# Scales of a weight matrix from sums of absolute values on ScalarE, where maxima on VectorE gave them

## The chip, the cores and the metric

The kernel runs on one core of a Trainium2 chip. The core has five engines, which run side by side and wait for each other through semaphores: TensorE (PE, matrix products; its weight loads are listed apart as PEld), VectorE (DVE), ScalarE (ACT), GpSimd (POOL) and SyncE (SP, which here issues nearly all DMAs). Each engine takes its instructions from a queue, in order. The metric is the time of one execution on the device in microseconds, lower being better, as a median over runs.

## The reference

Local and global attention for 8 sequences with 8 heads, followed by a feed-forward network:

```
k_all, v_all = concat(k_g, k_l), concat(v_g, v_l)        # 32 global + 512 local keys, head size 64
out_g = softmax(q_g @ k_all.T / 8) @ v_all               # 32 global queries see all
s     = concat(q_l @ k_g.T / 8, where(|i - j| <= 32, q_l @ k_l.T / 8, -1e9))
out_l = softmax(s) @ v_all                               # 512 local queries
x = concat(out_g, out_l) as [4608, 512]
h = x @ w_in                                             # w_in [512, 2048]
g = where(h > 0, h, exp(min(h, 0)) - 1)
return g @ w_out                                         # w_out [2048, 512]
```

The activations are float32; the two weight matrices come as float64.

## The kernel before

**Precision.** The two products of the network are done in f16, with each float32 operand split into a high and a low f16 part, and three products (high x high, high x low, low x high). For the split an operand is first divided by a power of two, so that it fits the range of f16. `unit` does it for one slice of weights: `power` keeps the exponent bits of a measure of the slice's size, `inverse` makes the reciprocal of it times a constant, ACT writes the high part (L216) and DVE the low part (L219). The powers stand in `pww` (for w_in) and `pwo` (for w_out), and every later scale is computed from them: `tables` multiplies the two and takes the largest product of a group of slices, `scales` makes from it the factors that are applied to the network's values. So any power of two that is large enough gives a correct split, as long as these tables use the same one.

**The weights.** Both matrices are read as pairs of 32-bit words (they come as float64), 1 MB at a time: eight slices of w_in and eight of w_out, in turn, w_in first. Each such slice is one `unit`. `fetch` loads it into the tile `raw`, of which there are two buffers, so the fetch of one unit waits until all instructions on the raw tile of the unit two before are done. A unit's steps are:

- s0: ACT takes absolute values of the high words (L188), POOL clamps them (L189);
- s1a, s1b, s1c: DVE builds the float32 number from high and low words (L193, L196, L200); the last reads the raw low words;
- s1d: the size of the slice. For w_in (m == 0) DVE takes the maximum of the absolute values in each partition (L205). For w_out ACT takes absolute values, writes them over the raw low words, and sums them in each partition on the way (L207); the sum is at least the maximum, and it serves as the measure;
- s2: for w_in alone, PE transposes the column of measures and DVE takes its maximum over the partitions (`all_max`, L141 and L142), as one power is used for all rows of a slice of w_in;
- s3 and s4: the power, the high part (L216) and the low part (L219).

**Order.** The program is written as one long stream of steps. `attention` yields after each small piece of attention work, `ffn_stream` after each small piece of the network, and the loop at the end mixes the two by a table, `PACE`. Each piece advances a clock by one tick; `defer(n, fn)` puts a step n ticks later. A unit's steps are put 1 to 5 ticks apart in the lead (the first 66 pieces of attention, with no network work yet) and up to 9 ticks later, the size at 5 or 9; s2 follows 8 ticks (w_out) or 17 ticks (w_in) after the unit's start. Units start at fixed pieces in the lead (`UNITS`) and then after every 14 pieces (`CONV`). The fetch of a unit is written one unit ahead. From this stream a planner makes the queue of each engine: it goes by the order of the program, but lets a later instruction pass an earlier one that would not be ready by its model of costs. DMA issues of SyncE stand in one queue: k, q and v of the attention, the raw weights (L174), and partial outputs of the network (`od`, L443 and L462), as blocks of rows are begun before all weights are converted.

**Around the change.** While weights are converted, DVE also does the scores' mask and minimum (L783), the sums for softmax (L793, L794, L798), the transposed probabilities (L814 or ACT), the low part of x (L574), the ELU (L345) and the low part of g (L348), and adds partial outputs (L458). ACT does the exponentials of the scores (L789), three passes over h for the ELU (L336 to L338), the high part of g (L352) and of x (L571), and copies out of PSUM (L749 to L753, L862). PE does scores (L772, L706), transposes by an identity matrix (L812, L745 to L748, L141), the products with v (L856, L825, L892), and the network (L327, L450; from the moment that all weights are there, L485, with seven products in place of eight).

Of the kernel before, what the change touches and what calls it, by code (L numbers as in the profile page):

```python
# [10 lines left out]
F32 = mybir.dt.float32  # L11
F32R = mybir.dt.float32r
I32 = mybir.dt.int32
AF = mybir.ActivationFunctionType
ALU = mybir.AluOpType
AX = mybir.AxisListType
# [44 lines left out]
def attn_ffn(ctx: ExitStack, tc: tile.TileContext, qT, qgT, kT, vT, vgT, vpT, w_in, w_out, mask, out):  # L61
    nc = tc.nc
# [22 lines left out]
    def defer(n, fn):  # L85
        if n == 0:
            return fn()
        later.setdefault(now[0] + n, []).append(fn)
# [39 lines left out]
    def power(dst, src):  # L128

        dst = dst.bitcast(I32)  # L130
        nc.vector.tensor_scalar(dst, src.bitcast(I32), 0x7f800000, None, ALU.bitwise_and)
        nc.vector.tensor_scalar_max(dst, dst, LOW)

    def inverse(dst, src):

        nc.vector.tensor_scalar(dst.bitcast(I32), src.bitcast(I32), TOP, -1.0, ALU.subtract, ALU.mult)

    def all_max(dst, src):

        tp = ps_a.tile([P, 512], F32, name="pa")  # L140
        tc.keep_in_program_order(nc.tensor.transpose(tp[:, 0:P], src.to_broadcast([P, P]), ident))  # L141
        nc.vector.tensor_reduce(out=dst, in_=tp[:, 0:P], op=ALU.max, axis=AX.X)  # L142
# [34 lines left out]
    def unit(m, p, raw):  # L177
        f = slice(2 * p * P, 2 * (p + 1) * P)
        shape = [P, NC, 2 * P] if m == 0 else [P, 2, DM]
        parts = [w[:, :, f] for w in win] if m == 0 else [w[:, 2 * p:2 * p + 2, :] for w in wout]  # L180
        pw = (pww if m == 0 else pwo)[:, p:p + 1]
        u = ffn.tile(shape, F32, name="cu", bufs=3)
        mx = ffn.tile([P, 4], F32, name="cm", bufs=4)
        high, low = raw[..., 1], raw[..., 0]
        ui = u.bitcast(I32)

        def s0():
            nc.scalar.activation(u, high.bitcast(F32), AF.Abs)  # L188
            nc.gpsimd.tensor_scalar(u, u, FMAX, FMIN, ALU.min, ALU.max)  # L189

        def s1a():
            tc.keep_in_program_order(
                nc.vector.tensor_scalar(ui, ui, 3, 0x3ffffff8, ALU.logical_shift_left, ALU.bitwise_and))  # L193

        def s1b():
            nc.vector.scalar_tensor_tensor(out=ui, in0=high, scalar=-0x40000000, in1=ui,  # L196
                                           op0=ALU.bitwise_and, op1=ALU.bitwise_or)

        def s1c():
            nc.vector.scalar_tensor_tensor(out=ui, in0=low, scalar=29, in1=ui,  # L200
                                           op0=ALU.logical_shift_right, op1=ALU.bitwise_or)

        def s1d():
            if m == 0:
                nc.vector.tensor_reduce(out=mx[:, 0:1], in_=u, op=ALU.max, axis=AX.XY, apply_absolute_value=True)  # L205
            else:
                nc.scalar.activation(low.bitcast(F32), u, AF.Abs, accum_out=mx[:, 1:2])  # L207

        def s2():
            if m == 0:  # L210
                all_max(mx[:, 1:2], mx[:, 0:1])

        def s3():
            power(pw, mx[:, 1:2])
            inverse(mx[:, 3:4], pw)
            nc.scalar.activation(parts[0], u, AF.Copy, scale=mx[:, 3:4])  # L216

        def s4():
            nc.vector.scalar_tensor_tensor(out=parts[1].rearrange("p a b -> p (a b)") if m else parts[1],  # L219
                                           in0=u.rearrange("p a b -> p (a b)") if m else u, scalar=mx[:, 3:4],  # L220
                                           in1=parts[0].rearrange("p a b -> p (a b)") if m else parts[0],
                                           op0=ALU.mult, op1=ALU.subtract)

        d = 1 if lead[0] else 2
        lag = 7 if m else 16
        for i, fn in ((1, s0), (1 + d, s1a), (1 + 2 * d, s1b), (1 + 3 * d, s1c), (1 + 4 * d, s1d),
                      (1 + lag, s2), (2 + lag, s3), (3 + lag, s4)):
            defer(i, fn)
# [848 lines left out]
```

## Time and profile before

| | |
|---|---|
| median of 3 runs | 960.44 us (958.44 to 963.3) |
| the profiled execution | 964.03 us |
| its span, first to last instruction | 962.2 us |
| PE, DVE, ACT, POOL busy | 914.8, 738.6, 661.9, 273.1 us |
| mean granted clock of TensorE | 0.97 |
| read from and written to HBM | 70.89 and 15.20 MB |

Times in the profile count from the start of the span. An engine is busy while it executes; waiting and issuing of DMAs are not counted. The granted clock is the share of TensorE's full clock that it was allowed in a stretch. In a timeline a row is start, length, engine, line, operation, what is written and read, shapes, and in brackets the idle time of the engine before it and the instruction that ended it. The chain of waits is followed back from the last instruction, at each step to what released it. Lines such as L205 are those of the kernel before.

### The profile page before, as it was taken

Reading aid. Unit: us, or ns where it says so; the run is one execution under the profiler, and the core shown is the slowest. Engines: PE = TensorE matmul, PEld = TensorE weight load, DVE = VectorE, ACT = ScalarE, POOL = GpSimd, SP = SyncE. Lnnn points to the kernel's source line nnn. Section 1 sums busy time; section 2 is a strip of 40 time slices with the busy share of each in tenths; the row PEclk is TensorE's granted clock in tenths of the full one; section 3 lists DMA queues with packets and bytes.
Section 4 is the critical chain, followed back from the end, with each engine's and each line's share of the span. In section 5 each row is a group of like instructions: output and inputs, shape, how many; then the busy total and the mean of one; then the engine's idle time right before and its main releaser. Section 6 shows DMA issues by size and latency. Waiting matters only on the chain.

```text
span 962.2 us, 23824 instructions
## 1 busy us (share of the span) xinstructions
PE 914.8 (95%) x9216; PEld 730.1 (76%) x9216; DVE 738.6 (77%) x2033; ACT 661.9 (69%) x1568; POOL 273.1 (28%) x483
## 2 busy tenths in 40 slices
PE   5887889899999999999999999999999999999997
PEld 2655566566666788788888888888888888888886
DVE  4877889989977876778776868687777877676566
ACT  4666788775676767757776866776776767666564
POOL 3636275372632212221221212222242222110000
PEclk7779899989999999999999999999999999999999
DMA  7852676622343114101230023001410101000000
GB/s 266 276 178 91 228 256 219 209 78 67 121 145 109 41 59 141 48 26 45 90 134 25 25 99 121 27 27 52 148 68 25 46 24 34 1 23 23 1 23 22
DMA packets 41769, 87.64 MB, mean 91 GB/s; under 512 B 7736, under 2 KB 8888, under 8 KB 41656
## 3 DMA queue, kind: packets, MB, share of 16 engines
q1 hardware_dynamic: 41368, 85.85, 26.4%
q8 instruction: 73, 1.20, 0.5%
q14 instruction: 40, 0.33, 0.1%
q10 hardware_dynamic: 288, 0.26, 0.1%
HBM read 70.89 MB, written 15.20 MB: 89 GB/s over the span
## 4 chain that ended last, share of the span: by engine, by line
PE 67%; DVE 17%; ACT 8%; issue 3%; POOL 3%; DMA 1%; DVEq 0%; SPq 0%; ACTq 0%; POOLq 0%
PE pa L327 25%; PE acc L485 12%; PE h L485 9%; PE pa L825 4%; PE acc L450 3%; PE pa L772 3%; PE h L327 3%; PE pa L812 2%; ACT p L789 2%; DVE gl L348 2%; PE pa L892 2%; DVE cu L278 1%; POOL p L796 1%; PE pa L706 1%; DVE cu L196 1%
## 5 line engine op out<-in xcount | busy, mean ns | idle before, releaser
L327 PEld LDWEIGHTS <-winh 128*128 128x128 f16 x2160 | 210.0, 99 | 42.0 <-issue 10.8
L796 POOL TENSOR_SCALAR p<-p,sm 128x128 f32<-128x128 f32 x256 | 144.1, 580 | 317.8 <-DVE sm L794 167.2
L327 PE MATMUL pa<-xh,winh 128*128 128x256 f16 x824 | 224.9, 273 | 0.1
L327 PE MATMUL pa<-xh,winl 128*128 128x256 f16 x824 | 224.6, 273 | 0.0
L327 PE MATMUL pa<-xl,winh 128*128 128x256 f16 x824 | 224.6, 273 | 0.0
L364 ACT ACTIVATE gh<-gx,xs 128x896 f16<-128x896 f32 x103 | 107.3, 1042 | 123.2 <-DVE gx L361 123.1
L348 DVE SCALAR_TENSOR_TENSOR gl<-gx,xs,gh 128x896 f16<-128x896 f32 x103 | 119.5, 1160 | 60.0 <-ACT gh L364 59.1
L485 PEld LDWEIGHTS <-gh 128*128 128x128 f16 x1456 | 139.6, 98 | 24.0 <-issue 7.4
L789 ACT ACTIVATE p<-p,m 128x160 f32<-128x160 f32 x256 | 106.6, 420 | 42.9 <-DVE m L783 41.3
L327 PEld LDWEIGHTS <-winl 128*128 128x128 f16 x1080 | 106.4, 99 | 14.5 <-issue 1.2
L336 ACT ACTIVATE g<-pa,xs 128x512 f32<-128x512 f32 x103 | 70.4, 683 | 24.1 <-PE pa L327 23.4
L485 PE MATMUL acc<-wouth,gh 128*128 128x256 f16 x312 | 85.2, 273 | 0.0
L485 PE MATMUL acc<-woutl,gh 128*128 128x256 f16 x312 | 85.0, 273 | 0.0
L485 PE MATMUL acc<-wouth,gl 128*128 128x256 f16 x312 | 85.0, 273 | 0.0
L338 ACT ACTIVATE g<-g 128x512 f32<-128x512 f32 x135 | 85.0, 630 | 0.0
L485 PEld LDWEIGHTS <-gl 128*128 128x128 f16 x728 | 71.2, 98 | 9.2 <-DVE gl L348 1.0
L327 PE MATMUL h<-xh,winh 128*128 128x256 f16 x256 | 71.9, 282 | 4.1 <-ACT hs L337 3.1
L485 PE MATMUL h<-raw,gh 128*128 128x256 f16 x416 | 75.0, 273 | 0.0
L327 PE MATMUL h<-xl,winh 128*128 128x256 f16 x256 | 71.8, 281 | 0.7 <-DVE xl L574 0.7
L327 PE MATMUL h<-xh,winl 128*128 128x256 f16 x256 | 71.8, 281 | 0.0
L783 DVE CUSTOM_DVE_ANT_0 p<-pa,msk 128x160 f32<-128x160 f32 x228 | 61.0, 317 | 7.1 <-PE pa L772 5.3
L345 DVE SCALAR_TENSOR_TENSOR gx<-g,hs 128x512 f32<-128x512 f32 x51 | 35.9, 705 | 36.0 <-ACT g L338 35.7
(237 smaller groups left out, 2028.8 us busy)
## 6 DMA issues: line engine op xcount, KB each, us to landing
k<-kT SPq DMA_DIRECT2D x32, 640.0 KB, 5.1
v<-vT SPq DMA_DIRECT2D x64, 256.0 KB, 2.7
q<-qT SPq DMA_DIRECT2D x32, 256.0 KB, 5.6
raw<-w_in SPq DMA_DIRECT2D x8, 1024.0 KB, 6.4
raw<-w_out SPq DMA_DIRECT2D x8, 1024.0 KB, 5.5
out<-o SPq DMA_DIRECT2D x32, 256.0 KB, 2.3
od<-o SPq DMA_DIRECT2D x24, 256.0 KB, 3.3
o<-od SPq DMA_DIRECT2D x24, 256.0 KB, 2.8
```

The source lines that it names most:

```text
L327: nc.tensor.matmul(h[:, j, :], wt[:, c, f], xt[:, c, :], start=k == 0, stop=k == 11)
L336: nc.scalar.activation(g, hf, AF.Relu, scale=sc[:, p:p + 1])
L338: nc.scalar.activation(g, g, AF.Exp, scale=-1.0)
L345: nc.vector.scalar_tensor_tensor(out=out, in0=ins[0], scalar=-1.0, in1=ins[1], op0=ALU.add, op1=ALU.max)
L348: nc.vector.scalar_tensor_tensor(out=dst, in0=src, scalar=sg, in1=hi, op0=ALU.mult, op1=ALU.subtract)
L364: nc.scalar.activation(gh, gx, AF.Copy, scale=sg)
L450: nc.tensor.matmul(acc[t], gt[:, s], wt[:, f, :], start=p == first and j == 0 and k == 0, stop=p == last and j == 1 and k == 2)
L485: nc.tensor.matmul(cols, gt, w, start=p == 0 and k == 0, stop=last and k == len(todo) - 1, skip_group_check=True)
L783: nc.vector.tensor_tensor_reduce(out=p, in0=sp[r][:, j * KW:(j + 1) * KW], in1=msk[:, mi, :], op0=ALU.add, op1=ALU.min, scale=-scale, scal ...
L789: nc.scalar.activation(ps[i], ps[i], AF.Exp, bias=m[:, i:i + 1], scale=-1.0, accum_out=s[:, 0, i:i + 1])
L796: nc.gpsimd.tensor_scalar(ps[i][:, 0:P], ps[i][:, 0:P], s[:, 1, i:i + 1], 1.0, ALU.mult, ALU.mult)
L825: nc.tensor.matmul(o[:, HQ * i:HQ * i + 96], v[:, 4 * i + h, :], x, start=False, stop=i == 1, skip_group_check=True)
```

## The change

For slices of w_in too, the size is now ACT's sum of absolute values per partition, written into the column of `mx` that the later steps read for this matrix (0 for w_in, 1 for w_out). The output of the elementwise operation goes over the raw low words, as it did for w_out. `all_max` then takes the maximum of the sums over the partitions. Nothing else is edited; the powers of two of w_in become larger, and with them all scales that are computed from them.

```
 def s1d():
-    if m == 0:
-        nc.vector.tensor_reduce(out=mx[:, 0:1], in_=u, op=ALU.max, axis=AX.XY, apply_absolute_value=True)
-    else:
-        nc.scalar.activation(low.bitcast(F32), u, AF.Abs, accum_out=mx[:, 1:2])
+    nc.scalar.activation(low.bitcast(F32), u, AF.Abs, accum_out=mx[:, m:m + 1])
```

## The prediction

> **What bounds the kernel now.** I read the page's header first, then the busy time by stretch, then the chain of waits, and last the timeline of each engine around the eight instructions that the change moves.
>
> ```profile
> span 962.2 us, 23824 instructions
> PE 914.8 (95%) x9216; PEld 730.1 (76%) x9216; DVE 738.6 (77%) x2033; ACT 661.9 (69%) x1568; POOL 273.1 (28%) x483
> ```
>
> TensorE is the bound: 914.8 of 962.2 us. What can be won lies in its 47 us of idle time and in time at a lower clock. The next rows give, for one stretch each: its length, busy us and instructions of PE, PEld, DVE, ACT and POOL, the granted clock, and the DMA share and rate.
>
> ```profile
> 100.00:150.00 50.00, 43.43 (x369) 28.74 (x367) 45.32 (x117) 42.21 (x95) 26.74 (x37) 0.90 0.69 231
> 150.00:200.00 50.00, 45.63 (x339) 28.48 (x338) 48.59 (x107) 38.28 (x81) 22.95 (x33) 0.93 0.56 185
> ```
> ```profile
> 250.00:962.00 712.00, 701.17 (x7374) 589.59 (x7372) 526.33 (x1434) 484.56 (x1120) 151.28 (x276) 1.00 0.17 58
> ```
>
> From 250 us on PE is busy for 701.17 of 712 us, at full clock. The weights are converted before that. There DVE is the fullest engine (48.59 of 50 us between 150 and 200, ACT 38.28), and PE is idle for 6.6 and 4.4 us of these two stretches. So DVE holds PE back there, and the moved instruction is part of it. Its rows, with shortest, median and longest duration in ns:
>
> ```profile
> L205 DVE TENSOR_REDUCE cm<-cu x8: 1183/1206/1214, 22.5 to 191.5; 128x1 f32<-128x1024 f32 x8
> ```
> ```profile
> L207 ACT ACTIVATE raw<-cu x8: 1132/1160/1210, 26.4 to 200.5; 128x1024 f32<-128x1024 f32 x8
> ```
>
> The chain that ended last (start, length, piece) goes through DVE's maximum at four of its eight places (the second to the fifth are not on it), and once through a fetch of w_in:
>
> ```profile
> 22.46 1.21 DVE cm L205
> ...
> 91.69 7.54 DMA raw<-w_in
> ...
> 154.23 1.13 DVE cm L205
> ...
> 171.45 0.99 DVE cm L205
> ...
> 191.56 1.13 DVE cm L205
> ```
>
> **The change, part by part: what DVE loses and ACT gains.** Instructions overlap at their ends, so the price is the distance from start to start. On DVE, around the first maximum, and on ACT, around the same work for w_out:
>
> ```profile
> 22.46 1.21 DVE L205 TENSOR_REDUCE cm<-cu 128x1 f32<-128x1024 f32 x1
> 23.59 1.21 DVE L196 SCALAR_TENSOR_TENSOR cu<-raw,cu 128x1024 int32<-128x1024 int32 x1
> ```
> ```profile
> 143.85 1.13 ACT L207 ACTIVATE raw<-cu 128x1024 f32<-128x1024 f32 x1
> 144.87 0.19 ACT L207 ACTIVATION_READ_ACCUMULATOR raw<-cu 128x1 f32 x1
> 144.96 1.13 ACT L188 ACTIVATE cu<-raw 128x1024 f32<-128x1024 f32 x1
> ```
>
> 23.59 - 22.46 = 1.13 us, and 144.96 - 143.85 = 1.11 us with the reading of the accumulator in it. So 8 x 1.13 = 9.0 us leave DVE and 8 x 1.11 = 8.9 us come to ACT. No DMA is added or removed.
>
> The Trainium skill has a rule against such a move: ScalarE: Activation LUTs, section "Rules for kernel authors", wants maxima and other simple arithmetic on VectorE, up to about 3 times faster in bf16. The trace does not agree for this f32 reduction, 1.13 against 1.11 us, and I give the rule no chance of its own. Were DVE three times as fast (1.13/3 = 0.38 us, an estimate from that page), the gain summed below would shrink from 3.8 to 1.3 us, and the change would come out 0.9 us slower.
>
> **What that is worth to PE.** PE's stalls behind DVE's maxima are these (in brackets the idle time and what ended it):
>
> ```profile
> 25.12 0.80 PE L856 MATMUL h<-ptg,ptw 128*64 128x160 f32 x4 [5.23 <-DVE ptg L756]
> ```
> ```profile
> 144.00 0.37 PE L327 MATMUL h<-xh,winh 128*128 128x256 f16 x1 [2.70 <-ACT hs L337]
> ```
> ```profile
> 162.83 0.38 PE L450 MATMUL acc<-wouth,gh 128*128 128x512 f16 x1 [0.89 <-DVE o L458]
> ```
> ```profile
> 192.35 0.58 PE L327 MATMUL h<-xh,winh 128*128 128x256 f16 x2 [0.84 <-ACT xh L571]
> 192.75 0.47 PE L141 MATMUL pa<-ident,cm 128*128 128x128 f32 x1
> 193.94 0.37 PE L327 MATMUL h<-xl,winh 128*128 128x256 f16 x1 [0.72 <-DVE xl L574]
> ```
>
> First maximum: PE waits 5.23 us for L756, which stands in DVE's queue behind L205 and L196. Without L205 it comes 1.13 us earlier: -1.1 us (-1.1 to 0, the latter if what follows then waits for a load).
>
> Second to fourth (near 39, 92 and 116 us): 0. DVE runs dry after each, so the time only moves into a wait for ACT, as this one after the third:
>
> ```profile
> 96.19 0.17 DVE L793 TENSOR_SCALAR sm<-sm 128x4 f32<-128x4 f32 x1 [1.55 <-ACT p L789]
> ```
>
> If that cover were gone, each would be worth up to 1.1 us.
>
> Fifth, by a row of DVE and one of ACT:
>
> ```profile
> 138.13 1.18 DVE L205 TENSOR_REDUCE cm<-cu 128x1 f32<-128x1024 f32 x1
> ```
> ```profile
> 142.66 0.72 ACT L352 ACTIVATE gh<-g,xs 128x512 f16<-128x512 f32 x1 [2.53 <-DVE g L345]
> ```
>
> PE's stall of 2.70 us ends with ACT's L337, behind L352, which waited 2.53 us for L345, which DVE reached only after L205 and what was queued between them. L345 moves up by 1.13 us and ACT has 2.53 us of idle time to take the new sum: -1.1 us (-1.1 to 0).
>
> Sixth: the stall of 0.89 us before L450, which waits for DVE, goes: -0.9 us (-0.9 to 0). Seventh and eighth: the stalls of 0.84 and 0.72 us near 192 us are one behind ACT and one behind DVE; L574 can start no earlier than ACT's xh is ready, so I take the one, -0.7 us (-1.6 to 0).
>
> Sum of the gains: -1.1 - 1.1 - 0.9 - 0.7 = -3.8 us.
>
> **What it costs.** ACT first. Where it stands idle for 2.53 us (above) or 4.99 us (below, before the second unit's sum), the new sum costs nothing; the sixth and the eighth find ACT with the evaluation of g and with xh in its queue. Both cost 1.11 us at most and nothing at least; I take half: +1.1 us. The transpose L141, which PE takes in order, now waits for ACT's sum; at 192.75 us it follows DVE's maximum (started at 191.56, 1.13 long) by 0.1 us, so this is the same wait behind another engine.
>
> ```profile
> 26.43 1.16 ACT L207 ACTIVATE raw<-cu 128x1024 f32<-128x1024 f32 x1 [4.99 <-DVE cu L200]
> ```
>
> Then a wait that the diff doesn't show. ACT's sum writes its elementwise output over the low words of the raw weights, where DVE's maximum wrote nothing. So a raw buffer of w_in comes free after the sum and not after L200, and SyncE's fetch two units on waits for it:
>
> ```profile
> 142.54 1.21 DVE L200 SCALAR_TENSOR_TENSOR cu<-raw,cu 128x1024 int32<-128x1024 int32 x1
> ```
> ```profile
> 152.42 1.21 DVE L200 SCALAR_TENSOR_TENSOR cu<-raw,cu 128x1024 int32<-128x1024 int32 x1
> ```
> ```profile
> 153.66 0.38 SPq L174 DMA_DIRECT2D raw<-w_in  x1
> 154.09 0.97 SPq L443 DMA_DIRECT2D o<-od  x2
> ```
>
> The L200 of 152.42 ends at 153.63, and w_in's fetch is issued at 153.66. It will go out at least 1.1 us later, plus what the sum waits in ACT's queue: the L207 quoted at 143.85 started 0.1 us after its L200 (142.54 + 1.21). I take 0.5 us, together 1.6 us (1.1 to 3.2, the upper end for a sum that waits for two others of its length, less the overlap). Behind the fetch in SyncE's queue stand other loads, here two of partial outputs that L458 adds at 162 us: 0. The fetched block itself is awaited by ACT, at the head of its in-order queue:
>
> ```profile
> 45.59 1.15 ACT L188 ACTIVATE cu<-raw 128x1024 f32<-128x1024 f32 x1 [1.12 <-DMA raw<-w_in]
> ```
> ```profile
> 99.24 1.14 ACT L188 ACTIVATE cu<-raw 128x1024 f32<-128x1024 f32 x1 [1.13 <-DMA raw<-w_in]
> ```
> ```profile
> 159.78 1.16 ACT L188 ACTIVATE cu<-raw 128x1024 f32<-128x1024 f32 x1 [0.41 <-DMA raw<-w_in]
> ```
>
> These three have no slack: 3 x 1.6 = 4.8 us of ACT's time. Behind them on ACT stand exponentials and g's high part, which PE needs only some microseconds later; I take a quarter, +1.1 us (0 to +4.8).
>
> Sum: -3.8 + 1.1 + 1.1 = -1.6 us. The profiled execution took 964.03 us (962.2 of it span, 1.8 around it), 3.6 us above the median of 960.44; -1.6 of 964.03 is 0.17%, so 960.44 becomes 958.8 us.
>
> **The rivals.** *A, the whole gain.* The costs stay hidden (-3.8), and the clock gains too. Two stretches at a granted clock of 0.50 lie behind two of the stalls:
>
> ```profile
> 143.70:147.10 3.40, 3.10 (x15) 2.16 (x15) 3.35 (x13) 3.26 (x6) 3.14 (x7) 0.50 0.29 29
> ```
> ```profile
> 191.50:198.30 6.80, 5.25 (x26) 3.40 (x25) 6.80 (x20) 3.79 (x15) 6.40 (x12) 0.50 0.00 0
> ```
>
> They cost half their length, 1.7 and 3.4 us. If shorter stalls avoid both: -3.8 - 5.1 = -8.9, 951.5 us. For it: four maxima on the chain, and DVE at 97%. Against: the second stretch starts after PE stalls of under 1 us, so that no stall is its evident cause. The Trainium skill, TensorE: Matmul & The Clock Gate, section "Why this matters for your kernels", has the clock fall after PE gaps of more than about 3 us; here it fell after 2.70 us and after less than 1, so that rows and rule differ. By the rule a shorter stall would save neither stretch, and this rival would end at -3.8, 956.7 us.
>
> *B, slower: the raw buffers become the bound.* Fetch, conversion, sum and release form a loop over two buffers. If each of the three fetches without slack is 3.2 us late and all of it reaches PE, because ACT stands at L188 with the exponentials behind it, that is +9.6; with -3.8 and +1.1 it makes +6.9, 967.3 us. It turns the sum positive from (3.8 - 1.1)/3 = 0.9 us per fetch on, if all of it reaches PE. For it: a fetch of w_in is on the chain for 7.54 us. Against: ACT, at 77% between 150 and 200 us, can catch up.
>
> *C, nothing arrives.* DVE's 9.0 us turn into waits for ACT, as after the third maximum: 0, 960.4 us.
>
> Beside these, the planner orders each engine's queue by modelled costs, so that other instructions may change places all along the kernel. No row prices that; it widens everything by some microseconds.
>
> **How the numbers follow.** The forecast 0.36, A 0.30, C 0.18, B 0.16. 0.5%, or 4.8 us, is about what a measurement of this kernel can tell from no change. Faster by more than that: A and a little of the forecast, 0.33. Slower: B and 0.01, 0.17. Within: 0.50. The range takes in A's time and nearly B's, 950 to 967 us; the forecast's own is 954 to 963.
>
> **What would show it.** Right: L205 gone from DVE, sixteen sums on ACT, the stall near 25 us down to some 4.1 us and the one near 144 us below 2 us, w_in's fetches issued right after ACT's sum. Wrong: ACT's waits for raw<-w_in at over 3 us each with longer PE stalls behind ACT (B); PE's idle time before 200 us unchanged (C); the low clock gone near 144 and 192 us (A); or a difference that lies after 250 us, where nothing here says one should.

## The result, and the profile after

The changed kernel takes 950.84 us (median of 6 runs, 948.65 to 954.98), against 959.44 us for the kernel before on the same chip: a ratio of 0.9898, 95% interval 0.9871 to 0.9925, which is faster by 1.0%, some 9.8 us (the two medians lie 8.6 us apart). A second comparison of the same two kernels, in the experiments, gave 0.9869 (0.9846 to 0.9891). The forecast was 958.8 us, a gain of 1.6 us. The profiled execution took 954.72 us, 952.9 of it span.

In the changed kernel the edit takes three lines away, so every line behind it has a number three lower: L204 is the sum (before L207), L753 the reduction that was L756, L853 the product that was L856, L324 was L327. The header of the page after:

```profile
span 952.9 us, 23830 instructions
PE 908.5 (95%) x9216; PEld 727.8 (76%) x9216; DVE 728.1 (76%) x2025; ACT 670.1 (70%) x1584; POOL 271.1 (28%) x483
```

The work moved as the diff says: DVE has eight instructions and 10.5 us less, ACT sixteen instructions (eight sums, eight readings of the accumulator) and 8.2 us more. But PE, whose 9216 instructions are the same, is busy for 6.3 us less, and that is the first sign of what was missed: between these two profiles its idle time shrank by only 3.0 us (47.4 to 44.4), and the rest of the difference is matmuls that ran faster.

To see where the time went, I cut each span where PE had done about the same number of matmuls (they stand in brackets behind PE's busy time), and asked for busy time by stretch. The columns are those of the prediction's tables: length, busy us and instructions of PE, PEld, DVE, ACT and POOL, the granted clock, DMA share and rate. Before:

```profile
0.00:42.70 42.70, 28.93 (x257) 17.80 (x261) 28.39 (x97) 21.73 (x68) 20.48 (x42) 0.74 0.77 268
42.70:89.10 46.40, 36.61 (x392) 24.22 (x385) 36.52 (x163) 32.50 (x121) 25.64 (x60) 0.83 0.44 145
89.10:133.90 44.80, 41.30 (x385) 27.82 (x385) 35.56 (x102) 35.66 (x87) 15.26 (x27) 0.92 0.70 241
133.90:212.00 78.10, 70.11 (x517) 45.85 (x514) 75.32 (x171) 61.34 (x120) 48.02 (x67) 0.93 0.53 174
212.00:962.20 750.20, 737.82 (x7681) 614.38 (x7679) 562.78 (x1502) 510.67 (x1175) 163.66 (x289) 1.00 0.18 60
```

After:

```profile
0.00:37.20 37.20, 25.81 (x255) 15.67 (x257) 23.72 (x88) 22.60 (x70) 17.15 (x36) 0.86 0.75 273
37.20:78.20 41.00, 36.41 (x387) 25.95 (x388) 34.44 (x166) 32.38 (x115) 27.91 (x63) 0.75 0.58 195
78.20:119.60 41.40, 38.02 (x387) 26.16 (x387) 37.81 (x106) 39.15 (x98) 19.04 (x33) 1.00 0.75 257
119.60:203.00 83.40, 70.91 (x518) 46.10 (x515) 69.73 (x170) 65.96 (x131) 43.48 (x64) 0.94 0.51 164
203.00:952.90 749.90, 737.39 (x7681) 613.93 (x7679) 562.36 (x1501) 510.01 (x1174) 163.51 (x290) 1.00 0.18 60
```

From 212 us on (203 after) nothing changes: 750.20 against 749.90 us. The first stretch gains 5.5 us, the second 5.4, the third 3.4. The fourth, which holds the fifth to the eighth slice of w_in and so most of the forecast's gains, *loses* 5.3 us. In this pair of profiles the kernel wins in the first 134 us, and gives more than a third of it back later. A profile is one execution, though. A second profile of each kernel (in the experiments) repeats the first three stretches, but there the fourth takes some 80 us before and after, so that the loss is not the rule. Length less busy time is PE's idle time: it falls by 2.4 us in the first stretch (13.8 to 11.4), by 5.2 in the second and by 0.1 in the third, and grows by 4.5 in the fourth. The busy time falls by 3.1 us in the first and by 3.3 in the third, where the clock is higher (0.86 for 0.74, 1.00 for 0.92).

The first stretch. PE's stall before the product with `ptg`, which was 5.23 us, and DVE's queue ahead of it, in the timelines of the changed kernel:

```profile
22.42 0.80 PE L853 MATMUL h<-ptg,ptw 128*64 128x160 f32 x4 [2.98 <-DVE ptg L753]
```
```profile
22.02 0.17 DVE L791 RECIPROCAL sm<-sm 128x4 f32<-128x4 f32 x1
22.11 0.26 DVE L753 TENSOR_REDUCE ptg<-pa 128x32 f32<-128x128 f32 x1
22.28 1.22 DVE L196 SCALAR_TENSOR_TENSOR cu<-raw,cu 128x1024 int32<-128x1024 int32 x1
```

The stall is 2.25 us shorter, twice the 1.13 us of the removed maximum. The cause can be read from the order of the rows. Before, DVE did the maximum (L205), then L196 of the next unit, and only then L756; now L753, the same reduction, comes ahead of L196. The planner made this queue anew once the maximum was gone, and a second instruction of 1.13 us slipped behind the one for which PE waits.

Stretches of half clock are the other part. In the kernel before they last 54.6 us in all in the first 200 us, after 41.0 (30.7 in the second profile). Two of those that remain:

```profile
39.20:52.90 13.70, 12.83 (x95) 8.64 (x99) 12.13 (x52) 10.40 (x38) 9.30 (x15) 0.50 0.80 281
182.50:189.30 6.80, 5.14 (x26) 3.19 (x23) 5.96 (x19) 4.83 (x19) 6.49 (x11) 0.50 0.00 1
```

The stretch near 144 us is gone, and the one that stood at 191.5 is still there, at 182.5 and as long as it was.

And the loss of the fourth stretch in this profile. Two lines of the list of waits of the changed kernel (engine, line, releaser: us, times, longest), and four rows of its timeline:

```profile
PE pa L141 <- ACT raw L204: 5.0, 4, 3.5
ACT cu L188 <- DMA raw<-w_out: 6.3, 4, 3.1
```
```profile
150.48 0.38 SPq L174 DMA_DIRECT2D raw<-w_out  x1
158.91 1.12 ACT L188 ACTIVATE cu<-raw 128x1024 f32<-128x1024 f32 x1 [3.09 <-DMA raw<-w_out]
160.53 1.13 ACT L204 ACTIVATE raw<-cu 128x1024 f32<-128x1024 f32 x1
161.80 0.32 PE L141 MATMUL pa<-ident,cm 128*128 128x128 f32 x1 [3.52 <-ACT raw L204]
```

ACT stands at the head of its queue for a block of w_out that landed late; behind it in that queue stands the new sum of w_in, and PE waits 3.52 us for the sum to be transposed. Before, PE waited 0.2 us in all for DVE's maxima at the eight transposes. A half-clock stretch of 3.4 us follows at once, at 162.0. Before, ACT waited 2.7 us for blocks of w_in and 0.3 us for blocks of w_out, in this list:

```profile
ACT cu L188 <- DMA raw<-w_in: 2.7, 3, 1.1
ACT cu L188 <- DMA raw<-w_out: 0.3, 1, 0.3
```

The first of these lines is missing from the list after: no wait for w_in's blocks is left, and the waits for w_out's have grown from 0.3 to 6.3 us. The late sums aren't the reason for that, since the kernels further below with the first slice or the first two on ACT, and DVE's maximum for the rest, have 4.7 and 5.4 us of these waits.

### The profile page after: what moved, and what is told of

It is laid out like the page before. It is cut to its first block, busy times and chain, and to the rows that moved or that the text cites. A ratio compares the mean times of both kernels' runs of the same rounds, so it can differ in the third digit from the quotient of the medians.

```text
span 952.9 us, 23830 instructions
## 1 busy us (share of the span) xinstructions
PE 908.5 (95%) x9216; PEld 727.8 (76%) x9216; DVE 728.1 (76%) x2025; ACT 670.1 (70%) x1584; POOL 271.1 (28%) x483
## 4 chain that ended last, share of the span: by engine, by line
PE 67%; DVE 14%; ACT 9%; POOL 3%; issue 3%; DMA 3%; SPq 0%; DVEq 0%; ACTq 0%; POOLq 0%
PE pa L324 25%; PE acc L482 12%; PE h L482 9%; PE acc L447 4%; PE pa L822 3%; PE h L324 3%; PE pa L769 3%; PE pa L809 2%; ACT p L786 2%; DMA raw<-w_out 2%; PE pa L889 2%; DVE gl L345 1%; POOL p L793 1%; DVE cu L196 1%; DVE cu L200 1%
## 5 line engine op out<-in xcount | busy, mean ns | idle before, releaser
L324 PEld LDWEIGHTS <-winh 128*128 128x128 f16 x2160 | 209.4, 98 | 39.2 <-issue 8.4
L793 POOL TENSOR_SCALAR p<-p,sm 128x128 f32<-128x128 f32 x256 | 147.8, 593 | 303.2 <-DVE sm L791 165.0
L324 PE MATMUL pa<-xh,winh 128*128 128x256 f16 x824 | 224.9, 273 | 0.1
L324 PE MATMUL pa<-xl,winh 128*128 128x256 f16 x824 | 224.6, 273 | 0.0
L324 PE MATMUL pa<-xh,winl 128*128 128x256 f16 x824 | 224.6, 273 | 0.0
L324 PEld LDWEIGHTS <-winl 128*128 128x128 f16 x1080 | 106.1, 98 | 14.3 <-issue 1.2
L324 PE MATMUL h<-xh,winh 128*128 128x256 f16 x256 | 71.1, 279 | 1.5 <-ACT hs L334 0.9
L324 PE MATMUL h<-xl,winh 128*128 128x256 f16 x256 | 71.0, 278 | 0.7 <-DVE xl L571 0.7
L324 PE MATMUL h<-xh,winl 128*128 128x256 f16 x256 | 71.0, 278 | 0.0
```

Of the source, the lines that this page charges most:

```text
L324: nc.tensor.matmul(h[:, j, :], wt[:, c, f], xt[:, c, :], start=k == 0, stop=k == 11)
L793: nc.gpsimd.tensor_scalar(ps[i][:, 0:P], ps[i][:, 0:P], s[:, 1, i:i + 1], 1.0, ALU.mult, ALU.mult)
```

## The experiments

All ratios are to the kernel before, on the same chip, with a 95% interval in brackets. Two rival theories stood at the start: the gain is DVE's relief all along the conversion (so it is spread over the eight slices), or it is something particular to a few places.

**The first slice alone.**

```
 def s1d():
-    if m == 0:
+    if m == 0 and p > 0:
```

Here and in the edits of this kind below, the `else` branch writes column `m` of `mx`, as in the change.

> Only the first of w_in's eight slices is measured by ACT's sum, the other seven keep DVE's maximum. Relief theory (DVE's queue held PE back, and every maximum that leaves it lets PE go on earlier): the stall of 5.23 us near 25 us shrinks to about 3.0 us as with the whole change, a low-clock stretch in the lead may go with it, and the end comes 2 to 4 us earlier, 955.5 to 957.5. Plan theory (the gain is that of another order of instructions, made from changed costs): the end may move either way, by as much as the whole change did.

Measured: 953.83 us, 0.9947 (0.9924 to 0.9971). One instruction in eight gives about half of the gain. Its timeline has the short stall already, and its first stretch, with 255 matmuls as in the tables above, is as short as that of the whole change:

```profile
22.38 0.80 PE L856 MATMUL h<-ptg,ptw 128*64 128x160 f32 x4 [2.97 <-DVE ptg L756]
```
```profile
0.00:37.20 37.20, 26.52 (x255) 16.11 (x257) 23.21 (x84) 22.64 (x70) 17.26 (x36) 0.82 0.74 271
```

Of the 5.5 us, 3.1 are idle time of PE (13.8 to 10.7) and 2.4 are busy time (28.9 to 26.5, the clock 0.82 for 0.74).

**All but the first.**

```
-    if m == 0:
+    if m == 0 and p == 0:
```

> The first slice of w_in keeps DVE's maximum, the other seven are measured by ACT's sum. Relief theory: what the first slice doesn't give is left, 5 to 7 us earlier than before, 952.5 to 954.5; the stall near 25 us is back at 5.2 us. Plan theory: no relation to the number of slices.

Measured: 957.45 us, 0.9973 (0.9953 to 0.9993), with the stall of 5.23 us unchanged. Seven of eight maxima moved, for a quarter of the gain. The theory of relief all along, which expected 952.5 to 954.5 us, is badly hit, and by the medians the two parts (5.1 and 2.6 us of 960) add up to less than the whole.

**Both: the sum on ACT, and DVE's maximum kept, into a column that nobody reads.**

```
+    nc.scalar.activation(low.bitcast(F32), u, AF.Abs, accum_out=mx[:, m:m + 1])
     if m == 0:
-        nc.vector.tensor_reduce(out=mx[:, 0:1], ...)
+        nc.vector.tensor_reduce(out=mx[:, 2:3], ...)
-    else:
-        nc.scalar.activation(...)
```

> The whole change, with DVE's maximum kept beside it: its result goes to a spare column that nobody reads. DVE gets its 9.0 us back, ACT keeps its 8.9 us more. Relief theory: the gain is gone, 958 to 964 us, the more so as ACT's sums now come on top. Plan theory, or a theory by which the sum itself (ready earlier than the maximum) gives the gain: 951 to 955 us stay.

Measured: 959.47 us, 0.9984 (0.9968 to 1.0001), the stall at 5.23 us. With the instruction back in DVE's queue no gain is left that the interval shows, so it is DVE's side that matters, and the sums bring nothing by themselves. ACT's extra work, which this kernel has too, shows no loss against the kernel before.

**A later release of the raw tile, taken away.** In the changed kernel the elementwise output of w_in's sum goes to the place of the high part, which is written later anyway, so that the raw tile comes free after L200, as before the change.

```
-    nc.scalar.activation(low.bitcast(F32), u, ...)
+    nc.scalar.activation(low.bitcast(F32) if m else parts[0], u, ...)
```

> The whole change, but ACT's elementwise output for w_in goes to the slice's place for the high part (which is overwritten later) and not over the raw low words, so that a raw buffer of w_in comes free after L200 again. Relief theory with a price of the later release (my +1.1 us): 1 to 3 us faster than the change, 948 to 950 us. If the later release costs nothing: 951 us, as the change. Rival B's price would be 5 us or more.

Measured: 952.42 us, 0.9915 (0.9887 to 0.9942), no better than the change. The later release costs nothing that can be measured, and ACT's waits for blocks of w_out are still there (7.3 us), so that it isn't their reason either.

**Less work on DVE, nothing on ACT.** The kernel before, with the maximum over 64 of 256 columns.

```
-    nc.vector.tensor_reduce(..., in_=u, ...)
+    nc.vector.tensor_reduce(..., in_=u[:, :, 0:64], ...)
```

> The kernel before with DVE's maximum over the first 64 of 256 columns only: three quarters of the reduction are left out (the maximum of a sample serves as the measure). DVE loses about 8 x 0.85 = 6.8 us, ACT gains nothing, and the raw buffers of w_in come free after L200 as before. Relief theory: at least as fast as the change, 948 to 953 us, as ACT pays nothing. A theory by which the gain needs ACT's sum or the new release of the raw buffers: 956 to 960 us.

Measured: 959.22 us, 0.9986 (0.9966 to 1.0007). The eight maxima take 0.33 us each from start to start in place of 1.13, and nothing comes of it:

```profile
23.90 0.80 PE L856 MATMUL h<-ptg,ptw 128*64 128x160 f32 x4 [4.43 <-DVE ptg L756]
```

The stall fell by the 0.80 us that was cut, since the queue kept its order. So DVE's busy time as such isn't the cause; relief all along had expected 948 to 953 us.

**A later transpose of the sums for three slices.** In the changed kernel PE takes L141 four ticks later for the fifth to seventh slice, so that it doesn't wait for ACT.

```
-    lag = 7 if m else 16
+    lag = 7 if m else 20 if 3 < p < 7 else 16
```

> The whole change, with the transposition of the sums and what follows it 4 ticks later for slices 4 to 6 of w_in. In the changed kernel PE stood 0.81, 0.33 and 3.52 us before these three transpositions, waiting for ACT's sum. If these waits are a price of the change: 2 to 4 us faster than the change, 947 to 949 us, with the waits gone. If PE only moves to another wait: 950 to 952 us.

Measured: 953.25 us, 0.9929 (0.9895 to 0.9964). The wait is nearly gone:

```profile
PE pa L141 <- ACT raw L204: 1.1, 2, 0.7
```

but the time is no shorter than the change's. With the early release as well:

> Both edits on top of the change: the release of w_in's raw buffers after L200, and the transpositions of slices 4 to 6 four ticks later. If both prices are real and add: 945 to 948 us. If one covers the other: as the better of the two.

953.36 us, 0.9926 (0.9904 to 0.9948). The wait of 3.52 us is one profile's; the second profile of the changed kernel has 2.6 us of it in all, the longest 1.4.

**A control: the maxima moved by one tick, nothing else.**

```
-    (1 + 4 * d, s1d)
+    (1 + 4 * d + (m == 0), s1d)
```

> The kernel before with the maxima of w_in put one tick later; no work is added, removed or moved between engines. Relief theory: 957 to 962 us, within 0.3% of before. Plan theory (any new order shifts the time by about as much as the change did): 4 us or more away from before, either way.

Measured: 961.97 us, 1.0017 (0.9998 to 1.0036), stall 5.23. So not any shuffle of queues makes this kernel faster. Its one profile, though, was 6 us shorter than that of the kernel before, with 34.1 us at half clock in place of 54.6, and all of that lead arises between 42 and 90 us: a single profile carries some microseconds either way, and only the ratios decide. That holds for the second stretch of the tables above too, whose 5.4 us one pair of profiles can't put down to the change.

**The order alone, for the first slice.** No work is moved; the first maximum is written four ticks later.

```
-    (1 + 4 * d, s1d)
+    (1 + 4 * d + 4 * ((m, p) == (0, 0)), s1d)
```

> The kernel before with the maximum of the first slice of w_in alone written four ticks later; no work is moved between engines. In the planner's queue of DVE the reciprocal L794 and the reduction L756, for which PE waits 5.23 us near 25 us, now stand ahead of L205 and of the second unit's L193 and L196. Order theory (the first slice's 5 us come from L756 passing the conversion steps, not from the 1.13 us of work): the stall falls to about 3 us, and the end comes 3 to 5 us earlier, 954.5 to 957. Work theory (DVE's 1.13 us have to go): within 1.5 us of before, 958 to 961.

Measured: 957.89 us, 0.9965 (0.9949 to 0.9982). Here the maximum still stands in DVE's queue, but behind L756:

```profile
21.71 0.26 DVE L756 TENSOR_REDUCE ptg<-pa 128x32 f32<-128x128 f32 x1
21.89 1.21 DVE L205 TENSOR_REDUCE cm<-cu 128x1 f32<-128x1024 f32 x1
```
```profile
22.02 0.80 PE L856 MATMUL h<-ptg,ptw 128*64 128x160 f32 x4 [2.37 <-DVE ptg L756]
```

The stall is shorter than in the changed kernel, and the ratio lies a little below 1 with DVE doing all it did, between the ranges of the two theories. But the trace doesn't let the stall be the reason. PE waits longer at two later places, and the first stretch is as long as that of the kernel before (42.70 us):

```profile
32.94 0.32 PE L141 MATMUL pa<-ident,wm_a 128*128 128x128 f32 x1 [1.50 <-ACT pg L723]
36.00 0.47 PE L812 MATMUL pa<-ident,p 128*128 128x128 f32 x1 [2.04 <-POOL p L796]
```
```profile
0.00:42.60 42.60, 28.07 (x253) 17.08 (x257) 27.64 (x97) 21.61 (x68) 19.81 (x42) 0.79 0.74 271
```

So the order shortens the stall by itself, and what was won there is waited off again before 43 us. Where the run's 0.35% comes from is open.

**The change again, and the kernel before again,** for a second profile of each.

> The changed kernel once more, on the chip of the run beside it: both theories expect the ratio of the first measurement, 0.987 to 0.9925, and a second profile shows how far the low-clock stretches differ between two executions of one program.

> The kernel before once more, one look: how far the low-clock stretches and the progress of PE in the first 200 us differ from its first profile (54.5 us at half clock). If the spread between profiles of one program is several us, single profiles can't carry differences of that size, and only the timed medians can.

Measured: 948.72 us, 0.9869 (0.9846 to 0.9891) for the change; 962.88 us in a single execution for the kernel before, within 2.2 us of its first profile at every matmul, with the same list of half-clock stretches. The two profiles of the change agree to within 2.2 us up to 158 us, differ by the wait of 3.52 us and the low clock behind it, and end 5.5 us apart.

**The first two slices.**

```
-    if m == 0:
+    if m == 0 and p > 1:
```

> ACT's sum for the first two slices of w_in, those of the lead; the other six keep DVE's maximum. Order theory (the gain is made where the order of the lead's queues changes and low-clock stretches go): close to the first slice alone, as the two programs differ in a few rows only, 0.993 to 0.996. Work theory (each maximum that leaves DVE where PE waits for it adds its share): the second slice adds nothing either, since DVE runs dry behind it. If the second slice adds 2 us or more, both miss how the lead works.

Measured: 949.84 us, 0.9876 (0.9854 to 0.9897). That is the whole gain; the other six slices, kept on DVE, are worth nothing that these intervals, some 0.3% wide to either side, can show. From the first slice alone to the first two the gain grows by 0.7%, so both theories missed. In PE's queue 14 of the 9216 matmuls stand at another place. First slice alone, around the second maximum:

```profile
37.39 1.20 DVE L205 TENSOR_REDUCE cm<-cu 128x1 f32<-128x1024 f32 x1
38.51 0.32 DVE L783 CUSTOM_DVE_ANT_0 p<-acc,msk 128x160 f32<-128x160 f32 x1
```
```profile
39.14 1.82 PE L772 MATMUL acc<-k,q 64*64 64x160 f32 x16 [1.65 <-DVE m L783]
41.12 0.91 PE L825 MATMUL h<-ptw,v 128*64 128x96 f32 x8 [0.17 <-DVE ptw L814]
```
```profile
37.20:82.30 45.10, 36.34 (x387) 25.34 (x386) 35.47 (x171) 31.05 (x113) 29.09 (x64) 0.77 0.55 179
```

First two slices:

```profile
36.89 0.30 DVE L783 CUSTOM_DVE_ANT_0 p<-acc,msk 128x160 f32<-128x160 f32 x1
```
```profile
37.51 1.25 PE L772 MATMUL acc<-k,q 64*64 64x160 f32 x16
39.49 0.55 PE L825 MATMUL h<-ptw,v 128*64 128x96 f32 x8 [0.74 <-DVE ptw L814]
```
```profile
37.20:76.30 39.10, 32.86 (x388) 23.10 (x387) 34.08 (x167) 31.96 (x115) 29.20 (x64) 0.91 0.60 206
```

The maximum stood right ahead of the score masks (L783) for which PE's next scores wait. Without it the stall of 1.65 us is gone, and the next one is 0.74 us in place of 0.17, so that the two together fall from 1.82 to 0.74 us, by about the length of the maximum. The same 387 matmuls then take 6.0 us less: 2.5 us of idle time and 3.5 us of busy time, as the clock is 0.91 in place of 0.77. At 37 us the two kernels were level. The better clock can't be put down to the second slice: the changed kernel, which has both sums on ACT as well, had 0.75 in this stretch in its first profile and 0.87 in its second.

**The first slice on ACT, and a quarter of the work for the other seven** (their maxima over 64 of 256 columns).

```
-    if m == 0:
-        nc.vector.tensor_reduce(..., in_=u, ...)
+    if m == 0 and p > 0:
+        nc.vector.tensor_reduce(..., in_=u[:, :, 0:64], ...)
```

> ACT's sum for the first slice, and for the other seven DVE's maximum over the first 64 of 256 columns only (three quarters of these reductions are left out). Work theory for what the first slice doesn't explain: DVE's queue has 7 x 0.85 = 6.0 us less and ACT nothing more, so the ratio is that of the whole change or better, 0.984 to 0.990. Order theory: as the first slice alone, 0.993 to 0.996.

Measured: 954.02 us, 0.9920 (0.9899 to 0.9942): between the first slice alone and the first two, outside the ranges of both theories, and not to be told from the former. The stall before the second slice's masks is nearly gone:

```profile
37.96 1.25 PE L772 MATMUL acc<-k,q 64*64 64x160 f32 x16 [0.38 <-DVE m L783]
```

Yet the time is 4.2 us longer than with the first two slices on ACT, on the same chip. In the two profiles PE is 1.4 us behind at 57 us and 5.1 us behind at 72 us, after waits of 2.87 and 2.72 us. Whether they come from what is left of the second maximum or from the other six, this run can't tell.

**The second maximum behind what PE waits for.** First slice on ACT; the second slice's maximum stays on DVE, two ticks later.

```
-    (1 + 4 * d, s1d)
+    (1 + 4 * d + 2 * ((m, p) == (0, 1)), s1d)
```

> The first slice's size is on ACT, as in the run that changed it alone; the second slice's maximum stays on DVE, two ticks later. Against that run the queues of PE, ACT, POOL and SP are the same, and in DVE's queue one instruction has moved: the maximum (L205) stands behind the four L783 for which PE waited 1.65 us at 39.14 us, and no longer ahead of them. If the place in DVE's queue is what the second slice's gain came from: the stall near 39 us falls below 0.6 us, the low clock that begins at 38.0 us goes or moves, and the time is about that of the run with both slices on ACT (0.9876 of the kernel before; 0.985 to 0.991). If it is the 1.13 us of work that must leave DVE: the stall goes but what stands behind the maximum is late instead, and the time stays near that of the first slice alone, 0.9947 (0.9925 to 0.997). In between, 0.991 to 0.9925, both have a part.

Measured: 955.63 us, 0.9930 (0.9909 to 0.9950). This lies in the range expected if the work must leave DVE (0.9925 to 0.997), at its fast end, and its interval stands clear of that of the first two slices. The trace shows that the place doesn't suffice here:

```profile
38.63 1.22 DVE L205 TENSOR_REDUCE cm<-cu 128x1 f32<-128x1024 f32 x1
```
```profile
38.28 1.82 PE L772 MATMUL acc<-k,q 64*64 64x160 f32 x16 [0.54 <-DVE m L783]
41.40 0.91 PE L825 MATMUL h<-ptw,v 128*64 128x96 f32 x8 [1.29 <-DVE ptw L814]
```
```profile
37.50:82.60 45.10, 36.45 (x388) 25.53 (x385) 35.55 (x171) 31.25 (x113) 29.33 (x64) 0.77 0.54 179
```

The stall before the scores falls from 1.65 to 0.54 us, and the copy L814, now behind the maximum, makes PE wait 1.29 us at its next product, where it had waited 0.17 us with the first slice alone. Together that is 1.83 us, where it was 1.82. The stretch has the same 45.10 us and the same clock of 0.77 to the last digit shown.

**The order alone, for both slices.**

```
-    (1 + 4 * d, s1d)
+    (1 + 4 * d + 4 * ((m, p) == (0, 0)) + 2 * ((m, p) == (0, 1)), s1d)
```

> The kernel before with no work moved to another engine: the first slice's maximum four ticks later (as in the run that measured 0.9965) and the second slice's two ticks later, behind the four L783. By the order theory the second place adds what it adds elsewhere, some 0.4 to 0.7%, and the time is 0.989 to 0.993 of the kernel before, which is most of the change's gain without the change. By the theory that the work must leave DVE, it stays at 0.9965 (0.995 to 0.998), since DVE has the same work.

Measured: 957.77 us, 0.9953 (0.9938 to 0.9969), not to be told from the first alone (0.9965). The further gain of the order theory didn't come. But the run tests it less than it was meant to: with the first sum on DVE, PE waits for neither masks nor copy between 39 and 48 us, in this kernel or in the one with the first maximum alone later, so there was no stall for the new place to remove. That the second maximum must leave the queue rests on the run before this one, where masks and copy both have PE waiting behind them and a new place only passes the stall on.

**All profiles side by side.** In the nine profiles of kernels with the first slice on ACT, the 256th matmul starts at 37.2 to 37.9 us; in the eight others, those with nothing but a new order among them, at 42.3 to 42.8. That is about 5 us for the first slice in every profile, and its timed ratio gives as much. From there, the next 387 matmuls take 45.3 us in both profiles with the second maximum whole on DVE, 43.4 with a quarter of it, and 39.3 to 42.7 in the six with the second sum on ACT. Where the first maximum is still on DVE that part takes anything from 39.9 to 46.6 us (40.4 in the control), so the second slice can be priced only beside kernels that have the first on ACT. None of the kernels beats the change clearly; the one with two slices is its equal.

## Why the prediction was wrong, by its own steps

The time lies at the edge of the range of 950 to 967 us, and the forecast gain of 1.6 us was six times too small. The direction was right, and so was the mechanism as far as it went, PE waiting behind DVE's maxima. What failed is the sizing of two terms: the sum put the first maximum at 1.1 us and the second at nothing, and the runs put them at 5.1 us (0.53%) and 6.8 us (0.7%). The other slices' terms are too small for the runs to show. There is also a slip in the sum: a quarter of 4.8 us is 1.2 and not 1.1 us, which moves the forecast by 0.1 us.

**"First maximum: -1.1 us": measured 5.1 us.** The stall fell by 2.25 us, as the planner put L753 ahead of the next unit's L196. "No row prices that; it widens everything by some microseconds", the prediction said of the planner. But one could have asked what the planner would do at this one place: two instructions of 1.13 us stood between PE and the one that it waited for, and the price of both was 2.3 us. The other half was a second omission. The prediction priced a stall by its own length; with the sum on ACT PE also waited some 0.8 us less at what follows and worked 2.4 us faster up to 37 us. The run with the order alone shows the reverse: its stall fell by 2.86 us, and at 43 us nothing of it was left.

**"Second to fourth: 0, DVE runs dry after each": the step that failed most.** It was read from the kernel before, where DVE did stand idle soon after the second maximum (and after the third; after the fourth only some 5 us later, for 0.40 us):

```profile
39.12 1.19 DVE L205 TENSOR_REDUCE cm<-cu 128x1 f32<-128x1024 f32 x1
40.23 0.31 DVE L783 CUSTOM_DVE_ANT_0 p<-acc,msk 128x160 f32<-128x160 f32 x1
```
```profile
42.84 0.22 DVE L869 TENSOR_TENSOR xglob<-xglob,h 128x64 f32<-128x64 f32 x1 [1.30 <-ACT xr L862]
```

The maximum stands right ahead of the masks here already. But PE has four groups of products (L856 and L825) before its next scores, which start at 42.3 us without a wait. With the first sum on ACT the planner put these scores behind the first of the four groups; then PE waits 1.65 us for the masks, and the second slice is worth 0.7% (0.9947 to 0.9876), more than any term of the sum. A cover was named with its price ("up to 1.1 us"), but it was held to be still there after the first step had made the queues anew. The stalls at this place fall by 1.08 us, so that even the price named was that of the stall and not of the time, which is six times as much; what makes up the rest no run shows.

**"Fifth -1.1, sixth -0.9, seventh and eighth -0.7": no net worth found.** With these slices left on DVE the time is the same as with all eight on ACT (0.9876 against 0.9898 and 0.9869). The forecast put their gains at 2.7 us and the costs of the change at 2.2 us, a net of 0.5 us, which is less than the runs can tell from nothing, so the single terms are neither borne out nor refuted. The fifth's mechanism is seen at its place: PE's stall behind ACT falls from 2.70 us to 0.93 (1.35 in the second profile). The half-clock stretch near 144 us did go, but not for that reason: it is gone too in the kernel with the first slice alone and in the control, where the same stall still lasts 2.68 and 2.70 us.

**ACT's +1.1 and the later fetch's +1.1: not found.** The kernel with the sum and the maximum did not come out slower than the one before, and the early release changed nothing. Nor does the move from DVE to ACT cost by itself: the rows give 1.13 against 1.11 us. The Trainium skill, ScalarE: Activation LUTs, "Rules for kernel authors", would keep a maximum on VectorE, up to about 3 times faster in bf16; the rows of this f32 reduction speak against it here, and the rule's case, bf16, no run here shows. Rival B is dead in the form in which it was told: w_in's fetches go out right after ACT's sum (one at 142.37 us after a sum that ends at 142.26), and yet the waits for w_in's blocks vanished. What did come is near it: ACT waits for w_out's block, the new sum stands behind that wait, and PE behind the sum (3.52 us in one profile, 1.4 at most in the other). The prediction had called L141's wait "the same wait behind another engine", at no cost; but an engine whose queue has a DMA wait at its head is not the same. The run that took this wait away gained nothing, so its price in the median stays open.

**Rival A had the size by luck, not by its places.** It gave 951.5 us; measured were 950.84. It put the clock's part at 143.7 and 191.5 us. In the profiles the clock's gain lies before 134 us; of the two places named, the second stayed, and the first went without the shorter stall. Its mechanism, that shorter stalls avoid half-clock stretches, fits the first stretch (3.1 us less idle, 2.4 us less busy with the first slice on ACT), but no run shows that the shorter stalls caused the better clock: with the second maximum only put behind the masks, the stall before them was 0.54 us, and the clock stayed at 0.77. The Trainium skill, TensorE: Matmul & The Clock Gate, "Why this matters for your kernels", ties the low clock to gaps of over about 3 us. In the kernel with the first slice alone half clock begins at 38.0 us, amid a stall of only 1.65 us, and with 0.54 us it begins at 38.6, so that rows and rule differ here too.

**Rival C held for six slices of eight, as far as the runs can tell.** PE's idle time did change, so it fell as a whole. But the third to the eighth maximum, and three quarters of the reduction in all eight (0.9986), are DVE time that was freed for nothing that shows.

**What stays open.** Why the second slice is worth 6.8 us when its stalls fall by 1.08; where the 0.35% of the order alone comes from; why the first and the other seven add up to less than the whole; and the exact condition for the lower clock.

## What to carry to other kernels

Price the removal of an instruction at its first place, then shift everything behind by what was won, and look again at the places that seemed covered: here the second place, worth nothing in the old profile, was worth more than the first. In a queue ordered by a planner, ask of every stall which other instructions could now pass, since an edit of one line shortened a stall by twice its length through a new order. And don't take a shorter stall for a gain: follow PE to a later matmul that both kernels share, since a new order alone shortened the same stall by more and was level again at the 256th matmul. And where an operation is moved behind an engine's DMA wait, what waits for it waits for the DMA too.

## What was unexpected of the hardware

Up to 200 us half-clock stretches were always multiples of 3.4 us long (3.4, 6.8, 10.2, 13.7, 17.1), and two profiles of the kernel before had them at the same places, within 0.5 us, with the same sum, 54.6 us. In a kernel whose PE is busy for 95% of the span, they took a quarter of the first 212 us. In every trace the clock changes on one grid of 3.41 us that runs through the whole span, and its place against the program differs between executions: the first stretch begins at 15.3 us in one profile of the change and at 14.3 in the other. They follow not only idle PE: the one at 191.5 us came after 3.4 us in which PE was busy for 0.71 of the time with the attention's small products and transposes. In the changed kernel the clock fell after the first of these two steps of the grid, where PE was busy for 0.80, and kept full speed after the second, with 0.43:

```profile
35.74:39.15 3.41, 2.73 (x34) 1.65 (x30) 3.41 (x19) 3.36 (x10) 1.62 (x5) 1.00 0.80 269
100.60:104.00 3.40, 1.46 (x6) 0.60 (x7) 3.40 (x5) 3.40 (x8) 0.00 (x0) 1.00 0.95 374
```

What decides I couldn't find.
